# Order of the first phase of an FNet and MoE kernel: first sequence folded before the weights, weights rounded per pair of chunks by VectorE and ScalarE

## Chip, cores, metric

One Trainium2 chip, one of its cores. The metric is the device time of one execution in microseconds (us), as a median of several runs.

## The reference, cut to what matters

```python
X = np.fft.fft(x, axis=1)            # x: [8, 3008, 256] float32
X = np.fft.fft(X, axis=2)
x = X.real.astype(np.float32).reshape(8 * 3008, 256)

h = x @ w_in                         # 256 x 2048, float64
r = np.maximum(h, 0.0)
g = r * r
out = (g @ w_out).astype(np.float32) # 2048 x 256, float64
```

The two weights arrive as float64. The chip has to round them to float32, and the kernel does that with integer and float operations on the two 32-bit halves of each number.

## The kernel before

The kernel folds `x` by symmetry on VectorE, in 7 tiles per sequence, and transforms the folded tiles on TensorE into `Pt`, `Qt` and `Et` (the products that make them are called the P, Q and E groups below; ScalarE's copy `da` and VectorE's joins `db` and `dc` lie between the products and these tiles). The second transform is multiplied into the weight once: `G1`, `G2` and `gE` are `w_in` times DFT tables. Then come 384 steps (8 sequences, 6 blocks of up to 251 columns, 8 pairs `j` of weight chunks). A step is `front` (TensorE products `ph`, from which VectorE makes `he` and then `g`), `combine` (ScalarE relu and square, GpSimd four sums) and, two steps later, `back` (TensorE products with `w_out`). The "first block" is the first 8 steps; in it one slice of `w_out` is rounded per step.

The program order before: round `w_in` and make G (4 turns), fold and transform sequence 0, then the steps.

```python
def rounded(dst, src):
    raw = sp.tile([P, 2, CH, 2], U32, name="raw", tag="s")     # CH = 256
    nc.sync.dma_start(out=raw..., in_=src.bitcast(U32))
    low, high = raw[:, :, :, 0], raw[:, :, :, 1]
    # nine VectorE operations, 128 x 512 each:
    # tensor_scalar, scalar_tensor_tensor, tensor_scalar, scalar_tensor_tensor, tensor_tensor,
    # tensor_scalar, tensor_scalar, scalar_tensor_tensor, scalar_tensor_tensor -> dst

WC = 512
for c in range(F // WC):                                       # 4 turns
    w = gp.tile([P, 2, WC], F32, name="win", tag="g")
    for i in range(WC // CH):
        rounded(w[:, :, i * CH:(i + 1) * CH], moe_w_in[...])
    for tab, G, n in ((cosd, G1, P), (sind, G2, P - 1)):
        ps = psh.tile([P, WC], F32, name="pg", tag="h")
        for i in range(2):
            nc.tensor.matmul(ps[0:n], tab[:, i], w[:, i], start=i == 0, stop=i == 1)
        nc.scalar.copy(G[:, cs], ps[0:n])
    ps = psd.tile([P, WC], F32, name="pe", tag="d")
    ...                                                        # eight one-column products
    nc.vector.tensor_copy(gE[:, ...], ps[:, 0:WC // P])
...
for _, f in ahead(0):                                          # fold and transform sequence 0
    f()
...
for i in range(len(steps) + LAG + 3):
    ...
    if i < NJ:
        load_wout(i)                                           # rounded(...) and four GpSimd sums
    g = front(b, k0, n, j, between)
    ...
    back(at[2], at[3], g_, s_)
    ...
    flight.append(((b, k0, n, j), g, combine(n, g)))
```

Tiles 0 and 1 of a sequence have 95 and 94 rows; the others 128, 60, 128, 128 and 120. Each engine executes its own program in the order in which the code issues to it.

## Time and profile before

| | before |
|---|---|
| time, median of 3 | 2125.74 us (2123.99 to 2126.36) |
| profiled span | 2124.2 us |
| TensorE busy, whole span | 95% |
| `ph` of step 8 starts (the first step that rounds nothing) | 191.59 us |
| VectorE busy up to then | 141.1 us (40.6 + 32.1 + 68.4) |

Read it from the bottom up: from step 8 on TensorE works without a gap, so everything that the change can win lies before 191.6 us, and there VectorE is busy for three quarters of the time and idle for 50.5 us. The lines themselves are in the prediction.

### The profile page before, as it was taken

What the parts mean: (1) busy time and instruction counts of PE and PEld (TensorE: products, weight loads), DVE (VectorE), ACT (ScalarE), POOL (GpSimd) and SP (SyncE); (2) the same over time, 40 slices, a digit from 0 to 9 for tenths busy, and PEclk for the clock granted to TensorE, in tenths of its full rate; (3) what the DMA queues carried; (4) which work ended last, traced back from release to release, by engine and by line L of the source; (5) the groups of instructions that cost most, each with busy time, mean ns of one, the idle gap of its engine ahead of it and who ended that gap; (6) DMA issues with size and microseconds to landing.
All of it is one profiled execution on the core that took longest, in us unless ns stands there. A gap on an engine that the chain in (4) does not pass through costs nothing.

```text
span 2124.2 us, 26994 instructions
## 1 busy us (share of the span) xinstructions
PE 2012.9 (95%) x9432; PEld 1740.2 (82%) x9432; DVE 1371.1 (65%) x3337; ACT 916.4 (43%) x1005; POOL 1223.2 (58%) x1797
## 2 busy tenths in 40 slices
PE   2567999999999999999999999999999999999998
PEld 1256888888888888888888888888888888888887
DVE  5689866677646775577656775577655776555553
ACT  0013444444444444454444454445444444444443
POOL 3036655566646764566655675567645666456665
PEclk7689999999999999999999999999999999999999
DMA  5212300010000110011001101001000100000000
GB/s 168 76 33 36 58 27 10 31 44 31 22 32 26 30 44 10 25 42 30 27 11 39 40 25 30 25 25 46 28 11 29 40 20 10 21 24 11 20 10 20
DMA packets 61729, 68.36 MB, mean 32 GB/s; under 512 B 25327, under 2 KB 49993, under 8 KB 61592
## 3 DMA queue, kind: packets, MB, share of 16 engines
q1 hardware_dynamic: 58392, 60.15, 9.8%
q0 software_dynamic: 2384, 6.22, 1.0%
q8 instruction: 74, 1.21, 0.2%
q14 instruction: 63, 0.52, 0.1%
q10 hardware_dynamic: 816, 0.26, 0.1%
HBM read 41.93 MB, written 24.68 MB: 31 GB/s over the span
## 4 chain that ended last, share of the span: by engine, by line
PE 92%; DVE 7%; ACT 0%; issue 0%; DMA 0%; POOL 0%; POOLq 0%; ACTq 0%; DVEq 0%
PE ph L377 15%; PE mA L417 15%; PE mC L417 15%; PE mB L417 15%; PE ph L378 15%; PE mD L417 7%; PE pd L317 6%; PE po L451 2%; PE pg L210 1%; DVE fs L196 1%; DVE fs L188 1%; DVE fd L187 1%; DVE fs L182 1%; DVE fs L194 0%; ACT os L453 0%; DVE fd L192 0%
## 5 line engine op out<-in xcount | busy, mean ns | idle before, releaser
L391 ACT ACTIVATE g<-g 128x1004 f32<-128x1004 f32 (+1 forms) x384 | 399.4, 1040 | 874.3 <-DVE g L383 575.9
L380 DVE SCALAR_TENSOR_TENSOR he<-Et,gE,ph 128x251 f32<-128x251 f32 (+1 forms) x768 | 362.0, 471 | 587.6 <-PE ph L378 586.9
L397 POOL TENSOR_TENSOR s<-g 128x251 f32<-128x251 f32 (+1 forms) x384 | 252.0, 656 | 687.2 <-ACT g L392 653.1
L377 PE MATMUL ph<-Pt,G 128*128 128x251 f32 (+1 forms) x1536 | 458.4, 380 | 29.3 <-DVE g L383 29.1
L378 PE MATMUL ph<-Qt,G 127*128 127x251 f32 (+1 forms) x1536 | 455.6, 377 | 0.0
L392 ACT ACTIVATE g<-g 128x1004 f32<-128x1004 f32 (+1 forms) x384 | 399.3, 1040 | 12.1
L417 PE MATMUL mA<-g,wout 128*128 128x251 f32 (+1 forms) x1536 | 391.2, 376 | 0.0
L417 PE MATMUL mC<-s,wsum 128*128 128x251 f32 (+1 forms) x1536 | 389.5, 375 | 0.0
L382 DVE TENSOR_TENSOR g<-he,ph 128x251 f32<-128x251 f32 (+1 forms) x768 | 320.5, 417 | 60.5 <-ACT g L392 1.5
L377 PEld LDWEIGHTS ph<-Pt,G 128*128 128x128 f32 x1536 | 290.0, 191 | 75.9 <-DVE g L383 35.8
L378 PEld LDWEIGHTS ph<-Qt,G 127*128 127x128 f32 x1536 | 294.5, 192 | 36.6
L417 PEld LDWEIGHTS mC<-s,wsum 128*128 128x128 f32 x1536 | 291.9, 190 | 34.8
L417 PEld LDWEIGHTS mA<-g,wout 128*128 128x128 f32 x1536 | 286.7, 190 | 39.9 <-issue 4.0
L383 DVE TENSOR_TENSOR g<-he,ph 128x251 f32<-128x251 f32 (+1 forms) x768 | 314.1, 409 | 0.0
L398 POOL TENSOR_TENSOR s<-s,g 128x251 f32<-128x251 f32 (+1 forms) x384 | 287.8, 750 | 30.1
L399 POOL TENSOR_TENSOR s<-g 128x251 f32<-128x251 f32 (+1 forms) x384 | 290.5, 757 | 0.0
L400 POOL TENSOR_TENSOR s<-g,s 128x251 f32<-128x251 f32 (+1 forms) x384 | 263.5, 686 | 0.0
L417 PE MATMUL mB<-g,wsum 128*128 128x251 f32 (+1 forms) x768 | 225.3, 374 | 0.0
L417 PE MATMUL mD<-s,wout 128*128 128x251 f32 (+1 forms) x768 | 225.2, 374 | 0.0
L417 PE MATMUL mB<-s,wout 128*128 128x251 f32 (+1 forms) x768 | 224.8, 374 | 0.0
L417 PEld LDWEIGHTS mB<-g,wsum 128*128 128x128 f32 x768 | 146.0, 190 | 17.7
L417 PEld LDWEIGHTS mD<-s,wout 128*128 128x128 f32 x768 | 145.1, 189 | 17.9
(75 smaller groups left out, 1320.9 us busy)
## 6 DMA issues: line engine op xcount, KB each, us to landing
out_dram<-os SPq DMA_DIRECT2D x96, 125.0 KB
xt<-in_x_dram SPq DMA_DIRECT2D x21, 512.0 KB
out_dram<-os SPq DMA_DIRECT2D x80, 126.0 KB
Et<-e_dram SPq DMA_DIRECT2D x7, 752.5 KB
raw<-in_moe_w_in_dram SPq DMA_DIRECT2D x8, 512.0 KB
raw<-in_moe_w_out_dram SPq DMA_DIRECT2D x8, 512.0 KB
xt<-in_x_dram SPq DMA_DIRECT2D x7, 480.0 KB
xt<-in_x_dram SPq DMA_DIRECT2D x7, 380.0 KB
```

Of the source, the lines that this page charges most:

```text
L377: nc.tensor.matmul(hP, G1[:, fs], pt[:, ks], start=True, stop=True)
L378: nc.tensor.matmul(hQ, G2[:, fs], qt[:, ks], start=True, stop=True)
L380: nc.vector.scalar_tensor_tensor(out=t, in0=et[:, ks], scalar=gE[:, fc:fc + 1], in1=hP, op0=ALU.mult, op1=ALU.add)
L382: tt(out=g[:, h, 0, 0:n], in0=t, in1=hQ, op=ALU.add)
L383: tt(out=g[:, h, 1, 0:n][:, ::-1], in0=t, in1=hQ, op=ALU.subtract)
L391: act(v, v, AF.Relu)
L392: act(v, v, AF.Square)
L397: gt(out=s1, in0=g21, in1=g22, op=ALU.add)
L398: gt(out=s2, in0=s1, in1=g11, op=ALU.subtract)
L399: gt(out=s3, in0=g11, in1=g21, op=ALU.subtract)
L400: gt(out=s4, in0=g12, in1=s2, op=ALU.subtract)
L417: nc.tensor.matmul(acc[nm][:, i, 0:n], w, v[:, 0:n], start=j == 0 and i == 0, stop=j == NJ - 1, skip_group_check=True)
```

## The change

Its intent: VectorE bounds the first phase, so take work off it and give it other work while it would wait. (1) A rounding is now five VectorE and three ScalarE operations, begun one rounding ahead and finished later. (2) Sequence 0 is folded and transformed first. (3) `w_in` is rounded per pair of 128-column chunks, two pairs before step 0 and one in each of the steps 0 to 5, beside `w_out`; the two roundings and the front of a step thus alternate with TensorE's products. (4) The first loads of `x` go through SyncE, the cosine tables through ScalarE.

```diff
     def load_x(b, t):
-        xt[b, t] = xp.tile([P, 4, D], F32, name="xt", tag="x")
-        (nc.sync if b else nc.gpsimd).dma_start(out=xt[b, t][0:rows], in_=x[b, ...])
+        pool, tag = (gp, "g") if b == 0 and t < NT - NX else (xp, "x")
+        xt[b, t] = pool.tile([P, 4, D], F32, name="xt", tag=tag)
+        nc.sync.dma_start(out=xt[b, t][0:rows], in_=x[b, ...])
...
+    FIRST = [*range(NT - NX, NT), *range(NT - NX)]        # tiles 4, 5, 6, 0, 1, 2, 3
+    for t in FIRST:
         load_x(0, t)
...
-                    nc.gpsimd.dma_start(out=tab[...], in_=src[...])
+                    (nc.scalar if tab is cosT else nc.gpsimd).dma_start(out=tab[...], in_=src[...])
...
+    def convert(dst, src):                                # cut: load of raw, low, high, m, e, ...
+        nc.vector.tensor_scalar(out=eb, in0=high, scalar1=20, scalar2=0x7FF, ...)
+        act(e, eb, AF.Relu, bias=ramp[:, 0:1], scale=-1.0)
+        act(eb, e, AF.Relu, bias=ramp[:, 1:2], scale=-2.0 ** 23)
+        nc.vector.tensor_scalar(out=mb, in0=high, scalar1=0xFFFFF, scalar2=0x100000, ...)
+        act(rest, low, AF.Copy, scale=2.0 ** -32)
+
+        def finish():
+            nc.vector.scalar_tensor_tensor(out=eb, in0=high, scalar=0x80000000, in1=eb, ...)
+            tt(out=m, in0=mb, in1=rest, op=ALU.add)
+            nc.vector.scalar_tensor_tensor(out=dst, in0=m, scalar=2.0 ** -20, in1=e, ...)
+        return finish
+
+    def load_win(j):
+        w = ep.tile([P, 2, CH], F32, name="win", tag="sB" if j % 2 else "sA")
+        finish = convert(w, pair_in(j))
+        def then():
+            finish()
+            ...                                           # pg products, G copies by ScalarE, pe products
+            nc.vector.tensor_copy(gE[:, j::NJ], ps[:, 0:2])
+        return then
...
-    for _, f in ahead(0):
+    ...                                                   # all sum folds, then difference folds and
+                                                          # groups in the order P, E, Q
+    weights = [lambda j=j: load_win(j) for j in range(2)]
+    for j in range(NJ):
+        if j + 2 < NJ:
+            weights.append(lambda j=j: load_win(j + 2))
+        weights.append(lambda j=j: load_wout(j))
+    begun = weights.pop(0)()
+
+    def next_weight():
+        nonlocal begun
+        then, begun = begun, weights.pop(0)() if weights else None
+        then()
+
+    for f in groups[16:20]:                               # first Q group
         f()
+    next_weight()
+    for f in groups[20:]:                                 # second Q group
+        f()
+    next_weight()
...
             if i < NJ:
-                load_wout(i)
+                for _ in range(2 if i + 2 < NJ else 1):
+                    next_weight()
+            if i == NJ:
+                for t in range(NX):
+                    load_x(1, t)
```

More of the change, by code (lines that the diff above doesn't have):

```diff
@@ L131, in load_x @@
         _, r0, step, rows = TILES[t]
-        xt[b, t] = xp.tile([P, 4, D], F32, name="xt", tag="x")
-        (nc.sync if b else nc.gpsimd).dma_start(out=xt[b, t][0:rows], in_=x[b, r0:r0 + step * (rows - 1) + 1:step])
+        pool, tag = (gp, "g") if b == 0 and t < NT - NX else (xp, "x")
+        xt[b, t] = pool.tile([P, 4, D], F32, name="xt", tag=tag)
+        nc.sync.dma_start(out=xt[b, t][0:rows], in_=x[b, r0:r0 + step * (rows - 1) + 1:step])
     cosd = const.tile([P, 2, P], F32, name="cosd")
@@ L145 @@
     gE = const.tile([P, NFC], F32, name="gE")
-    for dst, src in ((cosd, cos_d), (sind, sin_d), (altd, alt_d)):
-        nc.scalar.dma_start(out=dst, in_=src.rearrange("(c p) m -> p c m", p=P))
-    for t in range(NX):
+    FIRST = [*range(NT - NX, NT), *range(NT - NX)]
+    for t in FIRST:
         load_x(0, t)
-    for t, (c, r0, step, rows) in enumerate(TILES):
+    for t in FIRST:
+        c, r0, step, rows = TILES[t]
         for tab, src in ((cosT, cos_s), (sinT, sin_s)):
@@ L158 @@
                     nk = NC[0][c]
-                    nc.gpsimd.dma_start(out=tab[o:o + len(mine), :, PLACE[t]:PLACE[t] + nk],
+                    (nc.scalar if tab is cosT else nc.gpsimd).dma_start(out=tab[o:o + len(mine), :, PLACE[t]:PLACE[t] + nk],
                                         in_=src[mine[0]:mine[-1] + 1:step, :, i, 0:nk])
+    for dst, src in ((cosd, cos_d), (sind, sin_d), (altd, alt_d)):
+        nc.scalar.dma_start(out=dst, in_=src.rearrange("(c p) m -> p c m", p=P))
     make_identity(nc, ident)
-    def rounded(dst, src):
-        if src.dtype == F32:
-            nc.sync.dma_start(out=dst, in_=src)
-            return
-        raw = sp.tile([P, 2, CH, 2], U32, name="raw", tag="s")
-        nc.sync.dma_start(out=raw.rearrange("p a b w -> p a (b w)"), in_=src.bitcast(U32))
-        low, high = raw[:, :, :, 0], raw[:, :, :, 1]
-        def temp(tag):
-            t = fp.tile([P, 2, CH], F32, name=tag, tag=tag)
-            return t, t.bitcast(U32)
-        top, topb = temp("fs")
-        nc.vector.tensor_scalar(out=topb, in0=high, scalar1=3, scalar2=0x3FFFFFF8,
-                                op0=ALU.logical_shift_left, op1=ALU.bitwise_and)
-        nc.vector.scalar_tensor_tensor(out=topb, in0=high, scalar=0xC0000000, in1=topb,
-                                       op0=ALU.bitwise_and, op1=ALU.bitwise_or)
-        rest, restb = temp("fd")
-        nc.vector.tensor_scalar(out=restb, in0=topb, scalar1=0xFF800000, scalar2=None, op0=ALU.bitwise_and)
-        nc.vector.scalar_tensor_tensor(out=rest, in0=low, scalar=2.0 ** -52, in1=rest, op0=ALU.mult, op1=ALU.mult)
-        tt(out=top, in0=top, in1=rest, op=ALU.add)
-        over, _ = temp("fs")
-        _, expb = temp("fd")
-        nc.vector.tensor_scalar(out=expb, in0=high, scalar1=20, scalar2=0x7FF,
-                                op0=ALU.logical_shift_right, op1=ALU.bitwise_and)
-        nc.vector.tensor_scalar(out=over, in0=expb, scalar1=1150.5, scalar2=2.0 ** 127,
-                                op0=ALU.is_gt, op1=ALU.mult)
-        nc.vector.scalar_tensor_tensor(out=top, in0=expb, scalar=896.5, in1=top, op0=ALU.is_gt, op1=ALU.mult)
-        nc.vector.scalar_tensor_tensor(out=dst, in0=over, scalar=1.0, in1=top, op0=ALU.max, op1=ALU.mult)
@@ L200 @@
-    WC = 512
-    for c in range(F // WC):
-        cs = slice(c * WC, (c + 1) * WC)
-        w = gp.tile([P, 2, WC], F32, name="win", tag="g")
-        for i in range(WC // CH):
-            fs = slice(c * WC + i * CH, c * WC + (i + 1) * CH)
-            rounded(w[:, :, i * CH:(i + 1) * CH], moe_w_in[:, fs].rearrange("(c p) f -> p c f", p=P))
-        for tab, G, n in ((cosd, G1, P), (sind, G2, P - 1)):
-            ps = psh.tile([P, WC], F32, name="pg", tag="h")
-            for i in range(2):
-                nc.tensor.matmul(ps[0:n], tab[:, i], w[:, i], start=i == 0, stop=i == 1)
-            nc.scalar.copy(G[:, cs], ps[0:n])
-        ps = psd.tile([P, WC], F32, name="pe", tag="d")
-        for j in range(WC // P):
-            for i in range(2):
-                nc.tensor.matmul(ps[:, j:j + 1], w[:, i, j * P:(j + 1) * P], altd[:, i],
-                                 start=i == 0, stop=i == 1)
-        nc.vector.tensor_copy(gE[:, c * WC // P:(c + 1) * WC // P], ps[:, 0:WC // P])
@@ L219, in load_wout @@
-    def load_wout(j):
-        rounded(wout[:, :, j], moe_w_out.rearrange("(c j p) e -> j p c e", j=NJ, p=P)[j])
-        b11, b12, b21, b22 = (wout[:, c, j, h * H:(h + 1) * H] for c in range(2) for h in range(2))
-        t2, t3, t4 = (wsum[:, i, j] for i in range(3))
-        gt = nc.gpsimd.tensor_tensor
-        gt(out=t3, in0=b22, in1=b12, op=ALU.subtract)
-        gt(out=b12, in0=b12, in1=b11, op=ALU.subtract)
-        gt(out=t2, in0=b22, in1=b12, op=ALU.subtract)
-        gt(out=t4, in0=t2, in1=b21, op=ALU.subtract)
+    ramp = const.tile([P, 2], F32, name="ramp")
@@ new lines, with pair_in, pair_out @@
+    nc.gpsimd.memset(ramp[:, 0:1], 1151.0)
+    nc.gpsimd.memset(ramp[:, 1:2], 255.0 * 2.0 ** 23)
+    def pair_in(j):
+        return moe_w_in.rearrange("(c p) (h j f) -> j c p h f", p=P, j=NJ, h=2)[j]
+    def pair_out(j):
+        return moe_w_out.rearrange("(c j p) (o e) -> j c p o e", j=NJ, p=P, o=1)[j]
+    raws = 0
+    def convert(dst, src):
+        nonlocal raws
+        if src.dtype == F32:
+            for c in range(2):
+                nc.sync.dma_start(out=dst[:, c].rearrange("p (o e) -> p o e", o=src.shape[2]), in_=src[c])
+            return lambda: None
+        pool, tag = (xp, "x") if raws % (NX + 1) else (ep, "c")
+        raws += 1
+        raw = pool.tile([P, 2, CH, 2], U32, name="raw", tag=tag)
+        for c in range(2):
+            nc.sync.dma_start(out=raw[:, c].rearrange("p (o e) w -> p o (e w)", o=src.shape[2]),
+                              in_=src[c].bitcast(U32))
+        low, high = raw[:, :, :, 0], raw[:, :, :, 1]
+        m = fp.tile([P, 2, CH], F32, name="fs", tag="fs")
+        e = fp.tile([P, 2, CH], F32, name="fd", tag="fd")
+        mb, eb, rest = m.bitcast(U32), e.bitcast(U32), low.bitcast(F32)
+        nc.vector.tensor_scalar(out=eb, in0=high, scalar1=20, scalar2=0x7FF,
+                                op0=ALU.logical_shift_right, op1=ALU.bitwise_and)
+        act(e, eb, AF.Relu, bias=ramp[:, 0:1], scale=-1.0)
+        act(eb, e, AF.Relu, bias=ramp[:, 1:2], scale=-2.0 ** 23)
+        nc.vector.tensor_scalar(out=mb, in0=high, scalar1=0xFFFFF, scalar2=0x100000,
+                                op0=ALU.bitwise_and, op1=ALU.bitwise_or)
+        act(rest, low, AF.Copy, scale=2.0 ** -32)
+        def finish():
+            nc.vector.scalar_tensor_tensor(out=eb, in0=high, scalar=0x80000000, in1=eb,
+                                           op0=ALU.bitwise_and, op1=ALU.bitwise_or)
+            tt(out=m, in0=mb, in1=rest, op=ALU.add)
+            nc.vector.scalar_tensor_tensor(out=dst, in0=m, scalar=2.0 ** -20, in1=e, op0=ALU.mult, op1=ALU.mult)
+        return finish
@@ new lines, in load_win @@
+    def load_win(j):
[3 more added lines that the diff above has]
+            finish()
+            for tab, G, n in ((cosd, G1, P), (sind, G2, P - 1)):
+                ps = psh.tile([P, CH], F32, name="pg", tag="h")
+                for i in range(2):
+                    nc.tensor.matmul(ps[0:n], tab[:, i], w[:, i], start=i == 0, stop=i == 1)
+                nc.scalar.copy(G.rearrange("p (h j f) -> j p h f", h=2, j=NJ)[j],
+                               ps[0:n].rearrange("p (h f) -> p h f", h=2))
+            ps = psd.tile([P, CH], F32, name="pe", tag="d")
+            for h in range(2):
+                for i in range(2):
+                    nc.tensor.matmul(ps[:, h:h + 1], w[:, i, h * P:(h + 1) * P], altd[:, i],
+                                     start=i == 0, stop=i == 1)
+            nc.vector.tensor_copy(gE[:, j::NJ], ps[:, 0:2])
+        return then
@@ new lines, in load_wout, with then @@
+    def load_wout(j):
+        finish = convert(wout[:, :, j], pair_out(j))
+        def then():
+            finish()
+            b11, b12, b21, b22 = (wout[:, c, j, h * H:(h + 1) * H] for c in range(2) for h in range(2))
+            t2, t3, t4 = (wsum[:, i, j] for i in range(3))
+            gt = nc.gpsimd.tensor_tensor
+            gt(out=t3, in0=b22, in1=b12, op=ALU.subtract)
+            gt(out=b12, in0=b12, in1=b11, op=ALU.subtract)
+            gt(out=t2, in0=b22, in1=b12, op=ALU.subtract)
+            gt(out=t4, in0=t2, in1=b21, op=ALU.subtract)
+        return then
@@ L270, in f_d @@
             tt(out=new(fp, "fd", [P, 2, D])[r], in0=v[r, 0::2], in1=v[r, 1::2], op=ALU.subtract)
-            if b * NT + t + NX < B * NT:
+            if b > 0 and b * NT + t + NX < B * NT:
                 load_x(*divmod(b * NT + t + NX, NT))
@@ L286, in f_p @@
                 tt(out=wP[r, kp], in0=sc[r, 0], in1=sc[r, 1], op=ALU.subtract if kp else ALU.add)
+            folded[b, t, 0] = wP
         def f_q():
@@ L291, in f_q @@
                 tt(out=wQ[r, kp], in0=dc[r, 0], in1=dc[r, 1], op=ALU.add if kp else ALU.subtract)
-            folded[b, t] = (st["wP"], wQ)
+            folded[b, t, 1] = wQ
         return [(0.7, f_s), (0.7, f_d), (0.5, f_sc), (0.4, f_dc), (0.6, f_p), (0.6, f_q)]
@@ L313, in product @@
                     rows = TILES[t][3]
-                    w = we[t] if b is None else folded[b, t][which % 2]
+                    w = we[t] if b is None else folded[b, t, which % 2]
                     w = w[0:rows, kp]
@@ L355, in dft_ops @@
         ops = [] if b is None else [(0.0, start)]
-        for kp in range(2):
-            for which in ((2,) if b is None else (0, 1) if b else (0, 1, 2)):
+        for which in (2,) if b is None else (0, 1) if b else (0, 2, 1):
+            for kp in range(2):
                 ops += group(kp, which)
@@ L461, in ahead @@
         return ops + [(0.0, lambda: load_e(b))] if b else ops
-    for _, f in ahead(0):
-        f()
+    pieces = {t: [f for _, f in fold(0, t)] for t in FIRST}
+    for t in FIRST:
+        for i in (0, 2, 4):
+            pieces[t][i]()
+    first, *groups = [f for _, f in dft_ops(0)]
+    first()
+    for n, t in enumerate(FIRST):
+        for i in (1, 3, 5):
+            pieces[t][i]()
+        for f in groups[16 * n // NT:16 * (n + 1) // NT]:
+            f()
[10 more added lines that the diff above has]
+    for f in groups[16:20]:
+        f()
+    next_weight()
+    for f in groups[20:]:
+        f()
+    next_weight()
     LAG = 2
```

## The prediction

> **What bounds the kernel now.** I first read the page's rows of busy tenths.
>
> ```profile
> PE   2567999999999999999999999999999999999998
> DVE  5689866677646775577656775577655776555553
> PEclk7689999999999999999999999999999999999999
> ```
>
> One slice is 53 us. TensorE is full from slice 5 on; only the first four slices (212 us) are not its own. The change touches nothing after the first block of 8 steps, so the question is when TensorE gets full. The timeline of TensorE says when: the weight products of step 8 (`ph`, the first step that rounds no weights) start at 191.6 us, and from 197.8 us a step takes 4.68 us without a gap (11 matmuls of 0.425 us). What moves the start of step 8 moves the end of the kernel by the same amount.
>
> Next, the busy time of each engine in the three stages before that point and just after (columns: stretch, length, PE, PEld, DVE, ACT, POOL with counts, granted clock, DMA share, GB/s).
>
> ```profile
> 0.00:78.40 78.40, 30.41 (x96) 16.95 (x96) 40.63 (x76) 5.97 (x9) 18.65 (x33) 0.74 0.40 114
> 78.40:120.70 42.30, 28.93 (x90) 16.89 (x91) 32.09 (x100) 1.43 (x6) 2.25 (x4) 0.72 0.32 98
> 120.70:191.60 70.90, 41.71 (x145) 31.78 (x143) 68.35 (x119) 14.58 (x14) 38.54 (x59) 0.83 0.17 45
> 191.60:200.00 8.40, 8.40 (x33) 7.30 (x34) 5.70 (x14) 4.16 (x4) 5.10 (x8) 0.83 0.11 32
> ```
>
> Stage 1 rounds `w_in` and makes G: VectorE (DVE) and TensorE take turns. Stage 2 folds sequence 0 and transforms it. Stage 3 is the first block, with one `w_out` rounding per step: VectorE is 96% busy, a step takes 9.2 us (starts of `ph` at 136.3, 145.5, 154.7). The waits of VectorE up to 192 us show the turns of stage 1, four waits of about 7.8 us:
>
> ```profile
> DVE gE L217 <- PE pe L215: 31.1, 4, 8.6
> ```
>
> What ends there is the copy of `gE`, which stands in VectorE's program before the next rounding. The unit costs, by form and from TensorE's timeline:
>
> ```profile
> L188 DVE TENSOR_TENSOR fs<-fs,fd 128x512 f32<-128x512 f32 x16 | 12.8, 798 | 0.5
> L182 DVE SCALAR_TENSOR_TENSOR fs<-raw,fs 128x512 uint32<-128x512 uint32 x16 | 11.1, 692 | 0.6
> L180 DVE TENSOR_SCALAR fs<-raw 128x512 uint32<-128x512 uint32 x16 | 7.1, 443 | 5.1 <-DMA raw<-in_moe_w_in_dram 4.9
> 34.25 3.57 PE L210 MATMUL pg<-win,cosd 128*128 128x512 f32 x4 [10.82 <-DVE win L197]
> 37.66 1.88 PE L210 MATMUL pg<-win,sind 128*127 128x512 f32 x4
> L391 ACT ACTIVATE g<-g 128x1004 f32<-128x1004 f32 (+1 forms) x384 | 399.4, 1040 | 874.3 <-DVE g L383 575.9
> ```
>
> A one-source rounding operation costs 0.44 us, a two-source one 0.69 (0.80 as a mean, because beside GpSimd in stage 3 it takes 1.1). The same two 512-column products take 3.4 us after a gap (clock 0.5) and 1.7 at full clock. Last, the loads that SyncE issued at 91 us, tile 0 (95 rows) then tile 1 (94 rows), seen in one-microsecond windows:
>
> ```profile
> 94.00:95.00 1.00, 0.03 (x1) 0.00 (x0) 0.96 (x5) 0.00 (x0) 0.00 (x0) 0.50 0.32 131
> 96.00:97.00 1.00, 0.90 (x2) 0.00 (x0) 1.00 (x3) 0.00 (x0) 0.00 (x0) 0.50 0.17 49
> ```
>
> 131 GB/s at a share of 5/16, then 49 GB/s at about 2/16. This matters below.
>
> **What the Trainium skill says.** "DMA: Bandwidth & Descriptors", section "Why a DMA increments its semaphore by 16 and not by 1": a load issued by SyncE or ScalarE runs on the largest number of engines, up to 16, that divides its outer dimension. 95 gives 5, 94 gives 2: exactly the two lines above. "TensorE: Matmul & The Clock Gate", Part 1: idle and busy windows of about 3.4 us halve and restore the clock; the trace agrees (the first `ph` pair is slow after gaps of 4.05 and 3.94 us, fast after 2.27 and 2.44). "ScalarE: Activation LUTs", "What ACT_TABLE_LOAD costs": 186 ns + 0.833 ns per element, 93 more for a bias pointer; that is 1022 for 1004 columns, the trace has 1040. So I estimate 0.6 to 0.7 us for the new 512-column ScalarE operations.
>
> **The change, part by part.**
>
> *Rounding.* Nine VectorE operations become five, plus three on ScalarE. Before, start to start: 5.24 us (23.55 to 28.79 alone), 6.4 beside GpSimd. After: two one-source operations (0.46 each, start to start) begin it, three two-source ones (0.72 + 0.61 + 0.67 = 2.0) finish it: 2.92 us. 16 roundings x 2.3 = 37 us less VectorE, and some 8 x 1.2 = 10 us of the slowdown beside GpSimd, for VectorE will mostly wait while GpSimd combines. ScalarE's 1.9 us each run one rounding ahead: in a step 2 x 1.9 + two G copies (0.8) + 2.1 of its own is 6.7 us, under the step. I call it hidden.
>
> *Where the wait goes.* It is not removed. Each of the 8 pairs now has 256 columns: four products of 0.43 us (1.7) or at half clock 3.4, then the eight `pe` records (1.69/2 = 0.85), and VectorE still copies `gE` before it goes on: 2.7 to 4.4 us x 8, about 29 against 31.
>
> *First folding.* All 7 tiles now come through SyncE, while `cosT` and `sinT` come through two other queues. The engines 0 and 1 carry of x: 32 + 32 + 32 + 76 (380 KB over 5) + 188 (376 KB over 2) = 360 KB up to tile 1, 408 in all. At 25 GB/s per engine (131/5, 49/2) tile 1 takes 14.4 us; the tables in between, 190 KB per engine at 18 GB/s (288/16, what the tables alone had at 26 us), 10.6. From 2 us: tile 1 at 27, tiles 2 and 3 (two more us) at about 29, plus receipt. A sum fold is 1.55 us (0.61 + 0.54 + 0.41), so three of them after tile 1 end near 33.5. Until then VectorE has done 11 us of work: 22 us lie idle, where before it rounded from 4.9 us on. That is the price of the new order.
>
> *Then, VectorE in order* (in the brackets what each term is):
> - 33.5 to 53: 7 difference folds x 1.36 = 9.5, joins of four P and E groups x 2.0 = 8 (0.45 + 0.62 + 0.93 each), 2 of waiting for TensorE's first, slow group (6.3 us before, at 100 us).
> - to 56.5: the begin of the first weight 0.9, the Q group's joins, held by its odd product.
> - to 64: next begin 0.9 + finish 2.0, wait 4.4 (TensorE idle 4 us, so slow), `gE` 0.16.
> - to 68.6: second Q group (1.5 + 0.3 + 1.1 + 0.8 + 0.9); to 76: weight pair 1 as above.
> - step 0: 2.9 + 3.2 + 0.2 + 2.9 + front 2.3 (125.80 to 128.12 before) = 11.5, to 87.5.
> - steps 1 to 5: 8.3 + 0.3 contention + wait 3.6 = 12.2 each, 61, to 148.5.
> - step 6, one rounding: 5.5; step 7 up to the release of the first `ph` buffer: 2.0 + 1.2.
>
> Step 8 starts at 157.3 against 191.6: 34 us less. 2125.7 - 34.3 = 2091.4. The later blocks stay: the first loads of sequence 1 wait for a weight buffer that is free two steps before they are needed.
>
> **The rivals.**
>
> *A: the wait shrinks away and the gain is 45 to 55 us.* If TensorE stays warm the wait is 2.7 instead of 3.6 to 4.4 (about -11 us), and if x gets more than its share of the engines the folds end at 26 (-7): 2072. For it: x descriptors are 4 KB, the tables' 1.5 KB or less; a stage-3 TensorE was at 0.83. Against: between `back` and the next `pg` it idles 2.2 to 3.9 us (8.6 - 1.7 or 3.4 - 3.0), at the edge where the clock falls.
>
> *B: loads or ScalarE eat the gain.* If the tables finish after x, or the two-engine load of tile 1 runs slower than 24 GB/s, the folds end at 40; if strided 32-bit ScalarE reads take 1 us instead of 0.65, ScalarE needs 9 us of a 12 us step and still lags little. Together 8 to 12 us: 2102. For it: in the loads at 92 to 109 us engine 0 moved 360 KB in 17 us, 21 GB/s.
>
> *C: nothing, because the first phase was bound by loads anyway.* The start read 7.4 MB in 30 us (253, 232, 257 GB/s). But VectorE waited only 4.9 us for a load in all of it, so 2125 is unlikely.
>
> **Range and chances.** The two large unknowns are the wait per weight pair (8 x 0.9 us either way) and the end of the x loads (7 either way), with 3 to 5 us of small waits I have not counted: 2076 to 2104 around 2091. Faster by over 2% means under 2083.2, 8 us better than my sum: one in four. Slower by over 2% would need a step of over 20 us.
>
> **What would show it.** The profile after should have: `ph` of step 8 near 157; VectorE near 103 us busy before it; idle VectorE from 5 to about 29 us, ended by x loads, tile 1's the longest; `gE` <- `pe` waits of 8 times 2.7 to 4.4 us; steps 1 to 5 of 12 us. It is wrong if the folds end before 27 us, if ScalarE is what VectorE's finish waits for, or if a step of the first block takes under 11 or over 14 us.

## The result, and the profile after

The changed kernel takes 2100.86 us (2099.49 to 2102.47, four runs) against 2125.0 of before in the same rounds. The ratio is 0.9886 (0.9869 to 0.9903): 1.1% less, within 2%. Here and below a ratio is the mean time of one kernel's fast runs over that of the other's of the same rounds, so it is not quite the ratio of the medians quoted.

The rows of busy tenths, now with slices of 52 us:

```profile
PE   2689999999999999999999999999999999999997
DVE  4568856677557764677656775577646776555553
PEclk9779999999999999999999999999999999999999
```

TensorE is still not full in the first slices. `ph` of step 8 starts at 165.23 us instead of 191.59: 26.4 us earlier, and the profiled spans differ by 26.5 (2124.2 and 2097.7). The whole difference lies in the first phase.

Busy time by stage of the changed kernel (columns: stretch, length, PE, PEld, DVE, ACT, POOL with counts, granted clock, DMA share, GB/s). The stages are: sum folds; difference folds with the P and E groups; Q groups, the first two weight pairs and step 0; VectorE's steps 1 to 5; steps 6 and 7, up to step 8. The last two lines are one long step and one short step, by themselves.

```profile
0.00:38.70 38.70, 2.51 (x7) 1.56 (x7) 12.76 (x35) 1.28 (x1) 9.13 (x20) 1.00 0.69 181
38.70:57.70 19.00, 16.05 (x56) 9.16 (x56) 18.04 (x53) 0.95 (x4) 0.00 (x0) 1.00 0.27 83
57.70:95.50 37.80, 22.89 (x79) 17.22 (x78) 17.84 (x44) 12.62 (x23) 1.82 (x4) 0.73 0.18 56
95.50:156.20 60.70, 48.58 (x179) 40.59 (x180) 38.02 (x87) 33.45 (x50) 23.36 (x40) 0.75 0.24 73
156.20:165.20 9.00, 9.00 (x43) 7.69 (x42) 8.69 (x19) 6.08 (x7) 6.28 (x9) 1.00 0.26 83
98.27:111.37 13.10, 8.83 (x24) 6.93 (x25) 7.59 (x17) 6.73 (x11) 4.68 (x9) 0.63 0.27 81
124.47:135.07 10.60, 7.57 (x39) 6.50 (x39) 7.59 (x17) 6.64 (x11) 4.68 (x9) 0.96 0.35 101
```

VectorE's terms of the first five lines add up to 95.4 us, 45.7 less than before; but it is idle for 69.8 us (165.2 - 95.4) where it was idle for 50.5. So 19.3 of the 45.7 came back as idle time. In the long and the short step VectorE does exactly the same 7.59 us; only the granted clock differs, 0.63 and 0.96.

What VectorE waits for up to 165.2 us, in the changed kernel (total, times, longest):

```profile
DVE gE L236 <- PE pe L234: 37.2, 8, 5.4
DVE fs L292 <- DMA xt<-in_x_dram: 25.2, 5, 10.7
DVE db L357 <- ACT da L352: 3.5, 2, 2.0
```

The wait for `gE` has not shrunk with the work: eight waits of 4.65 on average in place of four of 7.8. The 25.2 us for the loads of `x` are new. In VectorE's timeline (start, duration, operation, idle before it):

```profile
20.76 0.69 DVE L292 TENSOR_TENSOR fs<-xt 95x512 f32<-95x512 f32 x1 [6.09 <-DMA xt<-in_x_dram]
33.36 0.69 DVE L292 TENSOR_TENSOR fs<-xt 94x512 f32<-94x512 f32 x1 [10.72 <-DMA xt<-in_x_dram]
60.51 0.25 DVE L357 TENSOR_TENSOR db<-da,pd 127x95 f32<-127x95 f32 x1 [2.01 <-ACT da L352]
```

Tile 1, the one of 94 rows, comes 12.6 us after tile 0. The third line is a wait that nobody had counted; ScalarE's timeline says what it was:

```profile
58.26 0.72 ACT L202 ACTIVATE fd<-fd,ramp 128x512 f32<-128x512 uint32 x1 [4.59 <-DVE fd L200]
59.08 0.72 ACT L203 ACTIVATE fd<-fd,ramp 128x512 uint32<-128x512 f32 x1
59.70 0.65 ACT L207 ACTIVATE raw<-raw 128x512 f32<-128x512 uint32 x1
60.26 0.22 ACT L352 COPY da<-pd 127x95 f32<-127x95 f32 x1
```

The little copy `da` of the Q group stands in ScalarE's program behind the three new rounding operations (0.72, 0.72, 0.65 us), and VectorE waits for it.

Last, TensorE's products of a weight pair in the long step and in the short one (the trace has two records for each product of the program):

```profile
98.27 2.08 PE L228 MATMUL pg<-win,cosd 128*128 128x256 f32 x4 [6.01 <-DVE win L213]
100.14 1.91 PE L228 MATMUL pg<-win,sind 128*127 128x256 f32 x4
101.84 1.71 PE L234 MATMUL pe<-altd,win 128*128 128x1 f32 x8
...
124.47 1.13 PE L228 MATMUL pg<-win,cosd 128*128 128x256 f32 x4 [1.03 <-DVE win L213]
125.44 1.03 PE L228 MATMUL pg<-win,sind 128*127 128x256 f32 x4
126.30 0.95 PE L234 MATMUL pe<-altd,win 128*128 128x1 f32 x8
```

After a pause of 6.01 us all three groups take nearly twice as long as after one of 1.03 us, the one-column `pe` products too. The five steps from 90.31 to 150.88 us (starts of `ph`) took 13.1, 13.1, 10.6, 13.1 and 10.7 us. From 150.88 us on, step 5, TensorE itself works without a gap (`ph` at 155.64, 160.31 and 165.23), so the last two steps before step 8 are no longer VectorE's alone.

### The profile page after: what moved, and what is told of

The parts are those of the page before. It is cut to its first block, busy times and chain, and to the rows that moved or that the text cites. A ratio compares the mean times of both kernels' runs of the same rounds, so it can differ in the third digit from the quotient of the medians.

```text
span 2097.7 us, 27091 instructions
## 1 busy us (share of the span) xinstructions
PE 2009.7 (96%) x9464; PEld 1747.5 (83%) x9464; DVE 1324.8 (63%) x3277; ACT 949.2 (45%) x1061; POOL 1209.7 (58%) x1780
## 3 DMA queue, kind: packets, MB, share of 16 engines
q0 software_dynamic: 752, 1.57, 0.3%
## 4 chain that ended last, share of the span: by engine, by line
PE 93%; DVE 4%; DMA 1%; ACT 1%; issue 0%; ACTq 0%; POOL 0%; POOLq 0%; DVEq 0%
PE mA L444 15%; PE ph L404 15%; PE mC L444 15%; PE mB L444 15%; PE ph L405 15%; PE mD L444 8%; PE pd L344 5%; PE po L478 2%; PE pg L228 1%; DMA cosT<-in_cos_s_dram 1%; DMA xt<-in_x_dram 1%; PE pe L234 0%; ACT os L480 0%; DVE fs L212 0%; DVE fd L210 0%
## 5 line engine op out<-in xcount | busy, mean ns | idle before, releaser
L419 ACT ACTIVATE g<-g 128x1004 f32<-128x1004 f32 (+1 forms) x384 | 399.4, 1040 | 12.1
```

The source lines that it names most:

```text
L419: act(v, v, AF.Square)
```

## The experiments

My theory after the result: the 8 us between the prediction (2091) and the measurement are the slow load of tile 1 and cold weight products, and the reason why a change that takes 46 us of work from VectorE brings only 26 is its order: it adds waits for loads and keeps the wait for `gE`. The rivals: the loads are bound by the total traffic, so cutting tile 1 differently gives nothing; what follows the pause hides it anyway; the rounding brings nothing by itself without the order. Line numbers differ a little between the kernels. All eleven kernels were correct.

The first four ran on one chip, with before at 2125.8 us.

### The two short tiles loaded in two parts

```diff
-        nc.sync.dma_start(out=xt[b, t][0:rows], in_=x[b, r0:...:step])
+        for a, e in ((0, 80), (80, rows)) if rows in (94, 95) and b == 0 else ((0, rows),):
+            nc.sync.dma_start(out=xt[b, t][a:e], in_=x[b, r0 + step * a:...:step])
```

> The changed kernel with the loads of tiles 0 and 1 of sequence 0 cut in two (80 + 15 and 80 + 14 rows), nothing else. In the trace of the changed kernel VectorE waits 10.7 us for tile 1 and the sum folds end at 38.7 us. Theory (the two-engine load of 94 rows is what the folds wait for): the 80-row part spreads over 16 engines, tile 1 lands near 24 us, the folds end at 27 to 31, step 8 starts 8 to 11 us earlier than 165.2 (154 to 157), the time is 2089 to 2093. Rival (the tables that load beside it are what takes the engines' time): the folds end at 36 to 39 and the time stays at 2098 to 2102.

Measured: 2094.95 us (2091.52 to 2098.02), ratio 0.9855 (0.9841 to 0.987). VectorE's timeline of this kernel:

```profile
26.08 0.69 DVE L293 TENSOR_TENSOR fs<-xt 94x512 f32<-94x512 f32 x1 [2.04 <-DMA xt<-in_x_dram]
...
71.21 0.55 DVE L358 TENSOR_TENSOR Qt<-dc,pd 127x376 f32<-127x376 f32 x1 [2.72 <-PE pd L345]
```

The fold of tile 1 starts 7.3 us earlier and the sum folds end at 31.9 instead of 38.7 us. So the rows of the load are the cause of these 7 us, for the bytes are the same. But they are not all of tile 1's lateness. SyncE's own waits before it issues the seven loads, in the changed kernel:

```profile
SPq L135 <- DMA cosT<-in_cos_s_dram: 18.0, 2, 16.5
SPq L135 <- DMA xt<-in_x_dram: 12.2, 2, 9.9
```

In its timeline cut into short windows, the load of tile 1, the fifth of the seven, is issued at 21.33 us only, after the wait of 16.5 us, and its fold starts 12.0 us later. With the load in two parts the larger part is issued at 20.89 us, nearly as late, and the fold starts 5.2 us after that. The rival was therefore half right: tile 1 also waits for the tables, but before its load is issued. Why the program lets SyncE wait there no run shows, and no experiment took this wait away.

In the profiled run step 8 came only 3.0 us earlier (162.19). The second line of VectorE's timeline shows part of where the rest went: the products of the second Q group took 6.80 us in that execution and 3.61 in the changed kernel's, and VectorE waited 2.7 us for them instead of 0.8. The fast case is the rarer one: in the profiles of six further runs in the new order, below, this wait is 2.5 to 3.4 us, and only in that of the last run is it 0.8 again. The theory holds for the load; of its gain of 6.8 us about 6 reach the median.

### The new order with the old rounding

```diff
     def convert(dst, src):        # begin: the load only
-        ...                       # two VectorE, three ScalarE operations
         def finish():
-            ...                   # three VectorE operations
+            ...                   # the nine VectorE operations of before
```

> The changed kernel with the nine-operation rounding of before, all on VectorE, in the new order. Theory (the cheaper rounding carries the whole gain and the new order costs something): each rounding costs 2.3 to 2.5 us more of VectorE, nearly all of it on its path, 16 x 2.4 = 38, less 1.5 for the ScalarE copy that no longer waits: 2135 to 2142, slower than the kernel before (2125). Rival (the order carries the gain, the rounding hides beside waits): 2100 to 2112.

Measured: 2154.14 us (2153.49 to 2157.68), ratio 1.0133 (1.0116 to 1.015). The direction of the theory, but 12 us beyond its range. Four of the five steps take 19.9 us, one 18.9. From VectorE's timeline of this kernel:

```profile
122.86 0.69 DVE L211 TENSOR_TENSOR fs<-fs,fd 128x512 f32<-128x512 f32 x1
...
130.28 1.11 DVE L211 TENSOR_TENSOR fs<-fs,fd 128x512 f32<-128x512 f32 x1
131.32 0.93 DVE L215 TENSOR_SCALAR fd<-raw 128x512 uint32<-128x512 uint32 x1
132.29 0.82 DVE L217 TENSOR_SCALAR fs<-fd 128x512 f32<-128x512 uint32 x1
...
140.24 0.16 DVE L243 COPY gE<-pe 128x2 f32<-128x2 f32 x1 [5.37 <-PE pe L241]
```

The same operation takes 0.69 us alone and 1.11 from 130.28 us, while GpSimd combines from 130.22 to 133.6. And the longer roundings leave TensorE idle so long that it is slow after them (5.37 us of wait in the step shown). The operations alone, 37 us by the prediction's count, would have made 2138 of 2101. Up to step 8, which starts 58.6 us later (223.81), VectorE is busy for 143.9 us against 95.4, 48.5 more and not 37, and its waits for `gE` are 41.0 us against 37.2; the other 6 us are not accounted for here.

### The new rounding in the old order

```diff
 (kernel before)
-            rounded(w[...], moe_w_in[...])
+            ends.append(rounded(w[...], moe_w_in[...], sp, "s"))     # begins: five operations
+        for end in ends:
+            end()                                                    # three more on VectorE
```

(With it, `w_out`'s roundings are begun one step ahead, and the loads of sequence 1 are moved to step 8 as in the change.)

> The kernel before, in its old order, with the new rounding begun one ahead (both halves of a 512-column chunk together; the second weight matrix one step ahead, in the buffers of x; the first loads of sequence 1 put off to step 8 for that). Theory (rounding carries the gain, order costs): a chunk of stage 1 goes from 18.1 to about 14.2 us (4 x 3.9 = 16), a step of the first block from 9.2 to about 5.8 (8 x 3.4 = 27): 2125 - 43 = 2082, clearly faster than the changed kernel. Rival (the rounding is hidden, the order carries the gain): 2118 to 2126.

Measured: 2102.33 us (2101.47 to 2102.67), ratio 0.989 (0.9875 to 0.9905): neither. VectorE's timeline of this kernel:

```profile
26.79 0.69 DVE L191 SCALAR_TENSOR_TENSOR fd<-raw,fd 128x512 uint32<-128x512 uint32 x1 [18.47 <-ACT fd L184]
```

and ScalarE's:

```profile
25.22 0.72 ACT L183 ACTIVATE fd<-fd,ramp 128x512 f32<-128x512 uint32 x1 [18.15 <-POOL ramp L165]
```

It is a flaw of my edit. In the old order GpSimd issues 24 table loads, and the two constants `ramp` that ScalarE needs were set behind them. The first finish waited 18.5 us. The run says nothing on the question; a mended one follows below.

### TensorE kept busy at the end of the first steps

```diff
+        if i < NJ - 2:
+            dummy = psd.tile([P, CH], F32, name="dm", tag="d")
+            for r in range(6 if i >= LAG else 13):
+                nc.tensor.matmul(dummy, ident, PQE[0][0][:, 0:CH], start=True, stop=True)   # unused
```

> The changed kernel with products that nothing reads, put at the end of steps 0 to 5 (13 in the first two steps, then 6, of 256 columns), so that TensorE does not pause long before the weight products. In the changed kernel steps of the first block take 13.1 us where the products run slowly and 10.6 where they run fast. Theory (the wait for the gE copy is long because TensorE's clock has fallen in the pause): waits of 5.0 to 5.4 us become about 3.1 in steps 1 to 5 and all take about 10.6 us; step 8 starts 5 to 9 us earlier, time 2092 to 2096. Rival (the slow and fast steps come from something else, such as GpSimd beside VectorE, or TensorE's own added work holds the steps): 2099 to 2106.

Measured: 2096.24 us (2094.35 to 2099.29), ratio 0.9863 (0.9848 to 0.9878). TensorE's timeline of this kernel, one step, and then VectorE's waits:

```profile
107.45 5.78 PE L565 MATMUL dm<-Pt,ident 128*128 128x256 f32 x26
113.62 1.13 PE L228 MATMUL pg<-win,cosd 128*128 128x256 f32 x4 [0.40 <-DVE win L213]
114.59 1.03 PE L228 MATMUL pg<-win,sind 128*127 128x256 f32 x4
115.45 0.95 PE L234 MATMUL pe<-altd,win 128*128 128x1 f32 x8
```

```profile
DVE gE L236 <- PE pe L234: 29.1, 8, 5.4
```

With work that computes nothing, every step takes 10.6 us (`ph` at 95.05, 105.66, 116.27, 126.91, 137.52, 148.19), and the five steps to 148.19 take 53.1 us instead of 60.6: 7.4 us that come with the clock, as the theory had it. From there to step 8 it is 16.7 us against 14.4, with the last six useless products among them, so that 5.1 us are left between the first `ph` and step 8 (69.8 against 74.9). In the time the gain is at the edge of what the intervals separate: step 0 began 4.7 us later in the profiled execution than in the changed kernel's, with the same program up to there; the products of the second Q group took 6.81 us in one and 3.61 in the other, and the waits that follow them make up 3.2 of the 4.7. When this happens no run settles, and it limits what differences of 3 to 5 us in this family can say.

The next four ran on another chip, with before at 2126.02 us.

### The copy of gE by ScalarE

```diff
-            nc.vector.tensor_copy(gE[:, j::NJ], ps[:, 0:2])
+            nc.scalar.copy(gE[:, j::NJ], ps[:, 0:2])
```

> The changed kernel with the gE copy of each weight pair on ScalarE in place of VectorE. VectorE's 8 waits for it sum to 37.2 us. Simple theory (these waits are lost time, all of it comes back where no other wait follows): 25 to 35 us less, 2066 to 2076. Rival (TensorE runs its program in order, so the ph products of the step stand behind the pair's products, and VectorE's front waits for ph instead): a step goes from 13.1 to about 12 and from 10.6 to about 9, in all 8 to 14 us less, 2087 to 2093, with a new wait of he for ph of 2 to 4 us per step.

Measured: 2085.86 us (2085.81 to 2086.26), ratio 0.9814 (0.9798 to 0.9831): 15 us better than the change by one word (by the 2% rule unclear against before), and about 1 us below the rival's range. VectorE's longest waits up to step 8 (151.8 us) in this kernel:

```profile
DVE fs L292 <- DMA xt<-in_x_dram: 24.4, 5, 11.0
DVE db L357 <- ACT da L352: 10.3, 2, 8.2
DVE he L407 <- PE ph L405: 2.9, 3, 1.0
DVE Qt L357 <- PE pd L344: 2.6, 1, 2.6
```

The 37.2 us of `gE` are gone. A part came back under other names: the second Q group's copy `da` needs that group's product, which stands in TensorE's program behind the pair's products (8.2 us for VectorE, once); the front waits for `ph`, which stands in TensorE's program behind the pair's products (2.9 us in all, much less than the rival's 2 to 4 per step). And the largest part is no wait at all. Up to step 8 VectorE is busy for 104.9 us here and 95.4 in the changed kernel, for it now rounds while GpSimd combines:

```profile
106.07 1.20 DVE L210 SCALAR_TENSOR_TENSOR fd<-raw,fd 128x512 uint32<-128x512 uint32 x1
```

The same operation took 0.68 us in the changed kernel, where VectorE waited for `gE` while GpSimd combined; a one-input operation just before goes from 0.42 to 0.94. The steps 1 to 5 take 10.0 us on average (87.84 to 137.73) instead of 12.1, and step 8 comes 13.4 us earlier, not 37.

### The pair of w_in finished after the front

```diff
-                for _ in range(2 if i + 2 < NJ else 1):
-                    next_weight()
+                next_weight()                  # w_out; the list now has it ahead of w_in
             g = front(b, k0, n, j, between)
+            if i + 2 < NJ:
+                next_weight()                  # the pair for step i + 2
```

> The changed kernel with each step's weight pair finished after the step's front instead of ahead of it (the second matrix's chunk first), gE still copied by VectorE. Theory (both the place of the products in TensorE's program and the gE copy on VectorE bind): the wait for gE only moves to the end of the step, 2097 to 2105. Rival (it is the place in TensorE's program alone that binds): 2075 to 2090.

Measured: 2111.72 us (2109.48 to 2114.26), ratio 0.9936 (0.9921 to 0.9951). Both theories fell; it is slower than the change. The step that starts at 128.99 us, in TensorE's timeline of this kernel:

```profile
135.41 2.04 PE L228 MATMUL pg<-win,cosd 128*128 128x256 f32 x4 [4.57 <-DVE win L213]
...
139.74 1.09 PE L444 MATMUL mA<-g,wout 128*128 128x251 f32 x4
```

`back` (the `mA` line begins it) now stands behind `pg`. In the changed kernel it filled TensorE's time while VectorE rounded; here TensorE is idle for 4.57 us in that time, is slow for `pg`, and does `back` afterwards, ahead of the next `ph`. The steps take 12.2 to 16.6 us. I had looked at VectorE's order alone.

### Both of these together, and with the loads in two parts

Edits: those of the last two sections; then the split loads as well.

> Both edits: the pair finished after the front, gE copied by ScalarE. Theory: nothing of VectorE's program waits for the pair's products any more; a step of the first block is VectorE's 8.3 to 9 us in place of 10.6 to 13.1, 5 x 3.3 + about 8 in step 0 and ahead of it: 2073 to 2082. Rival (TensorE at half clock or ScalarE becomes the bound): 2085 to 2095.

> The version that the theory asks for: the pair after the front, gE on ScalarE, and the loads of tiles 0 and 1 cut. If the savings add (loads 8 to 11, waits 20 to 26): 2064 to 2073, over 2% faster than before. If they don't (the earlier folds only lead into a slower, cold TensorE or into waits for weights): above 2075.

Measured: 2115.59 us (2113.81 to 2115.86), ratio 0.9952 (0.9937 to 0.9967), and with the split loads 2107.05 (2104.93 to 2108.36), 0.9913 (0.9898 to 0.9927). Both expected ranges of the first fell; the second is where its own rival put it, above 2075. The first's waits of VectorE up to 175 us:

```profile
DVE he L407 <- PE ph L405: 38.3, 8, 8.7
```

The wait that was `gE` (38.2 us up to 175 us in the run with the copy still on VectorE) has become, nearly to the microsecond, the wait for `ph`: `ph` stands behind the pair's products and `back`. Moving the copy does not remove the wait while the next operation of VectorE needs TensorE anyway. The split loads are worth 8.5 us here, and step 8 comes 7.3 us earlier (174.64 and 181.98): a second measurement of the load term, this time close to the 6.8 us of the folds.

The last three ran on a third chip, with before at 2126.64 us.

### The new rounding in the old order, mended

```diff
 (the new rounding in the old order)
+    ramp = const.tile([P, 2], F32, name="ramp")      # moved ahead of the table loads
+    nc.gpsimd.memset(ramp[:, 0:1], 1151.0)
+    nc.gpsimd.memset(ramp[:, 1:2], 255.0 * 2.0 ** 23)
```

> The new rounding in the old order again, with the two constants that ScalarE adds set by GpSimd ahead of its loads; in the run before they were set behind 24 table loads, and the first rounding waited 18.5 us for them. Theory (rounding carries the gain, the order costs): 2102.3 - 18.5 = 2084, between 2081 and 2087, clearly under the changed kernel (2101). Rival (the first 18 us of waiting hid a wait for weight loads that shows now): 2092 to 2102.

Measured: 2083.38 us (2082.08 to 2085.61), ratio 0.98 (0.9784 to 0.9816), as the theory had it (by the 2% rule unclear). Now the four combinations are known, in us, from runs in different rounds and on different chips, in all of which before took 2125 to 2127:

| | old rounding | new rounding |
|---|---|---|
| old order | 2126 | 2083 |
| new order | 2154 | 2101 |

The rounding alone is worth 42 us in the old order and 53 in the new. The order alone costs 28 us with the old rounding and 18 with the new. (The new rounding in the old order includes the edits that it needed: `w_out` begun one step ahead, the loads of sequence 1 at step 8.) The change is a good part and a bad part. The steps of the first block take about 6 us here instead of 9.2; what is left of the turns of stage 1 is in VectorE's waits up to step 8 (147.80 us):

```profile
DVE gE L219 <- PE pe L217: 29.5, 4, 7.6
```

### The old order without the turns

```diff
 (the last kernel, stage 1)
+    begun = begin_win(0)
+    for h in range(NH):                                  # halves of 256 columns
+        end, begun = begun, begin_win(h + 1) if h + 1 < NH else None
+        for o, p_ in outs:
+            nc.scalar.copy(o, p_)                        # G and gE of the chunk before
+        outs = []
+        end()
+        if h % 2:
+            outs = products(h // 2)
```

> The mended kernel in the old order with stage 1 taken apart: the next half of a chunk is begun before the last is finished, and ScalarE copies gE, one chunk late, so VectorE no longer waits for TensorE there. Theory (the 31 us of gE waits, with ScalarE's latency, are all that keeps stage 1 longer than VectorE's 8 x 2.8 us): stage 1 ends near 35 us instead of 66 to 79, time 2045 to 2060. Rival (the loads bound it: 4.2 MB of weights, 1.5 of x and 3 of tables at 250 GB/s are 35 us, and the second tables come last): 2060 to 2075.

Measured: 2063.37 us (2063.13 to 2063.54), ratio 0.9703 (0.9688 to 0.9717): faster than before by 3%, the best kernel. VectorE's waits up to step 8 (128.64 us):

```profile
DVE fd L181 <- DMA raw<-in_moe_w_in_dram: 17.8, 8, 5.0
DVE db L357 <- ACT da L352: 4.6, 5, 2.0
DVE Qt L357 <- PE pd L344: 3.4, 2, 2.7
```

No `gE` is among them: in stage 1 VectorE never returns to a result of TensorE before it has gone on with the next rounding. What it waits for now is the next load of `w_in`, which was the rival's bound, and the time lies in the rival's range, above the theory's; the last rounding of `w_in` ends at 40.5 us and not near 35. The DMA engines' share is 0.83, 0.88 and 0.99 in the first three stretches of 10 us. But SyncE also waits for VectorE to free a buffer before it issues a load (20.1 us in 5 waits up to 60 us), so whether more buffers would help is not tested.

### The new order, products of a pair behind the front

```diff
 (the changed kernel, with the gE copy on ScalarE and the split loads)
         def then():
             finish()
+            products.append(multiply)                    # pg, G, pe, gE: issued later
...
             g = front(b, k0, n, j, between)
+            while products:
+                products.pop()()
```

> The new order, with gE on ScalarE and the loads of tiles 0 and 1 cut, where each pair is still rounded ahead of the step's front but its products stand behind the front's ph in TensorE's program. Theory (what made the late pair slow is that the next ph stood behind products that had only just got their weights): VectorE no longer waits for ph, a step of the first block takes 8.5 to 9.5 us, 2065 to 2075. Rival (ph then waits for ScalarE's copies of the products, which share its two buffers): 2078 to 2095.

Measured: 2091.76 us (2090.24 to 2094.99), ratio 0.9838 (0.9824 to 0.9853). The size is the rival's, the mechanism is not quite. VectorE's waits up to 160 us:

```profile
DVE fd L212 <- ACT fd L205: 20.9, 6, 4.4
```

VectorE's finish waits for ScalarE's rounding operations, which stand in ScalarE's program behind copies of G and `gE` and behind relu and square. The wait has moved to the third engine. The one-word edit (2085.86) stays the better one in the new order, though that was on another chip.

## Why the prediction was right, and where it was off

The class and the range were right: 2100.86 lies in 2076 to 2104. The centre was 10 us too low, about 8 of it in the start of step 8 (165.2 against 157.3). By its own steps, as milestones of VectorE in us:

| end of | predicted | measured | added to the miss |
|---|---|---|---|
| sum folds | 33.5 | 38.7 | +5.2 |
| difference folds, P and E | 53 | 57.7 | -0.5 |
| first Q group | 56.5 | 62.6 | +1.4 |
| weight pair 0 | 64 | 70.3 | +0.2 |
| second Q group | 68.6 | 74.5 | -0.4 |
| weight pair 1 | 76 | 82.8 | +0.9 |
| step 0 | 87.5 | 95.5 | +1.2 |
| steps 1 to 5 | 148.5 | 156.2 | -0.3 |
| start of step 8 | 157.3 | 165.2 | +0.2 |

**First folding.** Half of the mechanism was right: tile 1 is the last that matters, and its 94 rows cost about 7 us, as the split loads show. The sum itself was not what happened. It has all seven loads under way from 2 us on, sharing the engines with the tables; in the trace tile 1's load is issued at 21.33 us, because SyncE waits 16.5 us for a load of `cosT` first. Nor was the rate off: between 29 and 33 us, when little else is loading, the windows show 47 to 53 GB/s, the 25 GB/s per engine of the prediction, so rival B's reason ("the two-engine load of tile 1 runs slower than 24 GB/s", folds at 40) is not the cause either, though its number was near. Tile 1 landed at 33.4 us and not at 27: that the sum missed by only 6 us is luck. The idle time of VectorE for `x` was 25.2 us against 22 predicted.

The second row of the table hides two errors that cancel: a difference fold takes 1.58 us from start to start and not 1.36 (1.5 us more for seven), and the wait for TensorE's first group was 0.2 us and not 2.

**Rounding.** VectorE does 95.4 us before step 8; I had said near 103. The two one-source operations take 0.34 us from start to start and 0.76 for both, not 0.92, and the slowdown beside GpSimd all but vanished in the `w_in` roundings (0.68 to 0.69 us). (VectorE mostly waits while GpSimd combines; without that wait, in the run with the `gE` copy on ScalarE, the slowdown is back.) ScalarE's operations take 0.72, 0.72 and 0.65 us, close to the estimate (0.6 to 0.7). That ScalarE is hidden was right within the steps, and wrong for the Q group: its copy `da` stands behind them, 2.0 us that the sum left out.

**Where the wait goes.** This step was right in its claim, that eight waits take the place of four and remove nothing, and wrong in its size: 37.2 us against about 29. The term that failed is the fixed 0.85 us for the `pe` products. At full clock they take 0.81 to 0.95, at half clock 1.57 to 1.71, so a cold wait is 4.9 to 5.4 and not 4.4. And six of the eight waits were cold (the other two 2.87 us), where the predicted mean of 3.6 stands for about half. The kept-warm run shows the clock's share: its five waits in the steps 1 to 5 are 2.87 us each. That its sum, 29.1 us, is the number predicted is chance, for its first three waits (5.37, 4.87 and 4.46 us) are cold or partly cold. And the reading of the pauses was too tidy: the prediction names four of them, but in the same trace the second `ph` pair was slow after pauses of 2.52 and 2.70 us, and in the changed kernel the weight products were slow after 2.98 and 3.04 us.

**Steps of 12.2 us.** The mean was 12.1, but by two errors that cancel: VectorE does 7.6 us and not 8.3 to 8.6, and waits 4.5 and not 3.6. And no step takes 12: they take 13.1 or 10.6, as the clock falls or not. A right sum is not yet a right account. The prediction called itself wrong if a step of the first block took under 11 us, and two of them did (10.6 and 10.7). The last row, +0.2, is right for another reason than the one given: TensorE is busy for all of those 9.0 us, VectorE for 8.7.

**Rivals.** A (45 to 55 us gained) needed a warm TensorE and early loads; neither came by itself. Each was then made, in part, by an experiment and gave about 5 to 8 us. B's number was the nearest to what happened. C is refuted: step 8 moved by 26.4 us.

What the prediction did not ask is whether the two halves of the change belong together. The four combinations answer it: the rounding alone would have brought 42 us, and the new order took 18 of them back. VectorE's waits up to step 8 show where: for loads at the start 25.2 us instead of 6.3 in the old order with the new rounding, for `gE` 37.2 instead of 29.5, for everything else 4.5 instead of 12.1, together 19 more.

What stays open: why SyncE's issues wait for other loads, and what the new order would take without that; and how much of the difference of a few microseconds between single executions is the clock. The run with the dummy products began step 0 4.7 us later than the changed kernel with the same program up to there, and no run here settles when that happens.

## What to carry to other kernels

An operation costs its duration and the place that it takes in its engine's program: price both, for every engine that the edit touches, because a wait that is moved to another engine comes back as that engine's next user (`gE` became `ph`, then `da`, then ScalarE's rounding). A wait that is removed can also let two engines slow each other down: VectorE was busy for 9.5 us more when it rounded beside GpSimd. For a load, look up when it was issued before you explain how long it took. When a change has two parts, time each part alone; here one part was worth 42 us and the other cost 18. And an engine that pauses for several microseconds does not only lose the pause: TensorE took nearly twice as long for what came after a pause of 6.01 us.

## What the Trainium skill lacked or had wrong

- "TensorE: Matmul & The Clock Gate", section "LDWEIGHTS (loading the stationary operand)", gives one figure for a weight load, columns divided by 1.2 in ns (107 ns for 128), without the clock. Here eight one-column records, each with its own weights, took 0.81 to 0.95 us at full clock (0.10 to 0.12 each) and 1.57 to 1.71 after a pause (0.20 to 0.21 each). The trace does not part the load from the product in them, but a model with a fixed cost was wrong by 0.8 us per pair.
- "SBUF — State Buffer", section "Who interferes with whom", says that a VectorE operation with two SBUF inputs and a GpSimd operation that reads SBUF exclude one another, and that a `tensor_scalar` in a two-port mode can contend too; it gives no figure for a row of such operations. Here 128x512 two-input operations went from 0.69 to 1.11 us beside GpSimd, and a one-input TENSOR_SCALAR from 0.42 or 0.43 to 0.93 or 0.82, a factor of 1.6 to 2.2 for the operations concerned. Whether the TENSOR_SCALAR ran in such a mode the trace does not say.
- "DMA: Bandwidth & Descriptors", section "Issuing engines are not separate DMA queues", calls the time that a sequencer takes to issue a DMA usually small relative to the DMA itself. That leaves out that issuing can itself wait. Here SyncE took 32.9 us to issue the seven loads of `x` (0.75 to 33.7), 30.2 of them in waits that ended with another DMA (18.0 with loads of `cosT`, 12.2 with loads of `x`), so that the first weight load behind them was issued at 33.7; and ScalarE took 23.4 us to issue twelve table loads.
